# Two-branch block: when a P.V. step's second part is issued, and where the softmax divisions stand

## The chip, the cores and the metric

The kernel runs on one core of one Trainium2 chip. The metric is the device time of one execution in microseconds; the median of 3 runs before the change is 2034.26 (2032.95 to 2034.44). The engines are PE (matrix multiplication), DVE (vector), ACT (activations and copies), POOL (element-wise work and masks) and SP, which here only issues transfers.

## What is computed

All inputs are float32; S = 2048 tokens, D = 576, 32 heads of 18, FH = 2304.

```python
xn = layernorm(x)
# branch A: sliding-window attention, window 256
q, k, v = heads(xn @ wqkv)
p = softmax(where(0 <= i - j < 256, q @ k.T * 18 ** -0.5, -1e9))
s = (p @ v) @ wo
# branch B: a gated MLP with a token mixer
z = gelu(xn @ w_in); z1, z2 = z[:, :FH], layernorm(z[:, FH:])
g = silu((z1 * (w_sp @ z2 + b_sp[:, None])) @ w_out)
out = x + s * g
```

## The kernel before

Every matrix product is made from operands split into a high and a low part, in two or three passes. The kernel goes through its stages in order: normalisation and the q, k, v and z2 products (to about 510 us of the profile), attention together with the z1 product (to about 1036 us), the out-projection (to about 1106 us), the token mixer (Strassen-like products, L1278 on) and the last product with w_out.

The change lies in the attention stage (L895 to L1013). Its work is cut into 16 units (`UNITS`, L24): 8 groups of four heads, first for the lower half of the tokens, then for the upper. For a unit `u` there are five kinds of work:

- maxima: `max_item` (L484) makes a block of scores on PE and takes its row maximum on DVE; 32 per unit. `max_split` and `max_end` (L506, L516) split the maxima into high and low, transpose them on PE, copy them on DVE (`mhl`) and move them by four transfers into rows of the q operand, so that the later scores come out with the maximum already subtracted. The scores of a unit wait for that move.
- scores: `scores` (L606) makes the transposed scores of one head and one key block on PE, ACT takes their exponential (L625), and POOL masks the two edge blocks of all four heads (L633, L636). When four heads are done, the key block goes to the list `todo`.
- P.V.: `pv` (L639) multiplies a key block with the values, for four heads, into an accumulator `ops` of which there is one (`bufs=1`) and which holds four query blocks (`c`). A key block whose queries reach over the end of an accumulator is done in two parts: the second part goes to the list `later` (L656). When an accumulator is full, ACT copies it into half of the tile `ou` (L662; two buffers), and the second parts get the planned end of that copy as their time (L664).
- the end of a unit: `finish` (L669). The values have a column of ones, so `ou` holds the denominators too. A transfer gathers them (`den`, L713), DVE takes the reciprocal (L676), a transfer writes it to memory (`r_d`, L679), another reads it back broadcast to all rows (`rp`, L685; one buffer), DVE multiplies the two halves of `ou` with it (L692; here called the division), and four transfers store the result (`o_d`, L702).
- fill: `z1_rows` (L556), the z1 product. Its matmuls use one half of PE's rows (`ma` or `mb`), as the scores and maxima do, so two run at a time. They are put in wherever nothing else is ready.

The order on all engines is written out by the kernel while it is built (`manual_schedule`). A planner (L962 on) keeps a clock and the planned busy time of ACT, DVE and POOL, and at each step emits what is due: functions registered with `after(ns, fn)` when the clock reaches them (`tick`, L462), then P.V. steps if `pv_now` says so, then a score or a maximum, else fill. Each engine executes its own list in the order in which the planner emitted it, and SP issues its transfers in that order too. So a planned time fixes only a place in the lists; on the chip an instruction waits at that place for what it needs, and what stands behind it waits too.

`pv_now` (L941) counts the entries of `todo` that are due, and `pv_run` (L948) takes that many from the head. After a step that ends an accumulator, the second parts are put at the head of `todo` (L956).

The last unit (u = 15) is treated apart: its tile is `oul`, and its division is made in the out-projection stage (L1052 on). The out-projection's weights are loaded and split during unit 15 (`load_wo`, L885), into buffers of `ou` and `vg` among others (L1003). The tokens' attention results are loaded back by `wo_load` (L872) into `spare` and the operand buffers of heads that are done, and split into `ohl` (L1030), whose memory was `ou` and others of the attention stage.

Of the kernel before, what the change touches and what calls it, by code (L numbers as in the profile page):

```python
# [42 lines left out]
GUARD = 150  # L43
LOAD_NS = 4000
MAX_NS = 3500
WARM = 54


# [9 lines left out]
def kernel(  # L58
# [14 lines left out]
    act, dve, pool, pe, sp = nc.scalar, nc.vector, nc.gpsimd, nc.tensor, nc.sync  # L73
# [154 lines left out]
    with ExitStack() as early:  # L228
# [5 lines left out]
        def pair_banks():  # L234

            turns.append(0)
            return [(fillp, widep)[len(turns) % 2].tile([P, 512], F32, name=n) for n in ("ma", "mb")]
# [6 lines left out]
        with ExitStack() as ph:  # L244
# [104 lines left out]
            warm_up = pair_banks()  # L349
            for n in range(WARM):  # L350
                pe.transpose(warm_up[n // 4 % 2][:, n % 4 * P:(n % 4 + 1) * P], ident, ident)
# [65 lines left out]
        with ExitStack() as ph:  # L417
# [34 lines left out]
            clock = 0.0  # L452
            row_time = [0.0, 0.0]

            def after(ns, fn):
                waiting.append((clock + ns, fn))

            busy = {"act": 0.0, "dve": 0.0, "pool": 0.0}
# [57 lines left out]
            def max_end(u):  # L516
# [14 lines left out]
                for i in range(4):  # L531
                    after(wait + 100 * i, lambda: to_move[u] and to_move[u].pop(0)())
                max_ready[u] = clock + wait + 400 + MAX_NS

# [64 lines left out]
            vgs, pts, left, o_ps, ous, last, todo, later = {}, {}, {}, {}, {}, [], [], []  # L599
# [39 lines left out]
            def pv(u, kb, qa, qz):  # L639
                g, half = UNITS[u]  # L640
                pt = pts[u, kb]
                k0 = 0 if half == 0 else 6
                c = qa // 4
                first = max(4 * c - 2, 0)
                if kb == first:
                    o_ps[c] = ops.tile([P, 512], F32, name="ops")
                hi = min(4 * c + 3, qz)
                for j in range(4):
                    pe.matmul(o_ps[c][32 * j:32 * j + 32, (qa - 4 * c) * P:(hi - 4 * c + 1) * P],  # L649
                              vgs[u][:, kb - k0, j * VW:j * VW + 32], pt[:, j, (qa - kb) * P:(hi - kb + 1) * P],  # L650
                              start=kb == first, stop=kb == 4 * c + 3, skip_group_check=True)
                spend_both((hi - qa + 1) * 218)
                if hi == qz:
                    pts.pop((u, kb))
                else:
                    later.append([0.0, u, kb, hi + 1, qz])  # L656
                if kb == 4 * c + 3:
                    if c % 2 == 0:
                        ous[u] = (ap_.tile([P, HS], F32, name="ou", bufs=2) if u < NU - 1 else
                                  aa.tile([P, HS], F32, name="oul", bufs=1))  # L660
                    ou = ous[u]
                    act.activation(ou[:, c % 2 * 512:c % 2 * 512 + 512], o_ps.pop(c), AF.Copy)  # L662
                    free_at = use("act", 630)
                    for t in later:  # L664
                        t[0] = free_at
                    if c % 2 == 1:
                        finish(u, ou)

            def finish(u, ou):  # L669

                g, half = UNITS[u]
                cs = slice(half * HS, half * HS + HS)
                den = aa.tile([P, HS // 32], F32, name="den")
                rp = ap_.tile([P, HS], F32, name="rp", bufs=1) if u < NU - 1 else f32(slots[4][:, 0:HS])
                def put_inverse():
                    dve.reciprocal(den, den)  # L676
                    t = use("dve", 350) - clock + 300
                    after(t if u < NU - 1 else 0,
                          lambda: sp.dma_start(r_d[u].rearrange("h (a b) -> (h a) b", b=HS // 32), den))  # L679
                    if u == NU - 1:  # L680
                        tick()
                    return t

                def get_inverse():
                    sp.dma_start(rp, r_d[u].unsqueeze(1).to_broadcast([4, 32, HS]))  # L685

                def invert():
                    after(put_inverse() + 4800, get_inverse)

                def divide_half(a):  # L690
                    hs = slice(a * 512, a * 512 + 512)
                    dve.tensor_tensor(ou[:, hs], ou[:, hs], rp[:, hs], ALU.mult)  # L692
                    use("dve", 750)

                def divide():
                    if u == NU - 1:
                        divide_half(0)
                    divide_half(1)

                    def store(i):  # L700
                        h = 4 * g + i
                        sp.dma_start(o_d[h * DH:(h + 1) * DH, cs], ou[32 * i:32 * i + DH, :])  # L702

                    for i in range(4):
                        if u == NU - 1:
                            store(i)
                        else:
                            after(busy["dve"] - clock + 200 + 400 * i, partial(store, i))

                if u == NU - 1:  # L710
                    last.extend([lambda: sp.dma_start(den, ou[DH::32, :]), put_inverse, get_inverse, divide])
                else:
                    after(busy["act"] - clock + 300, lambda: sp.dma_start(den, ou[DH::32, :]))  # L713
                    after(6000, invert)
                    after(16000, partial(divide_half, 0))
                    after(18000, divide)

            def sp_combos(stack):

# [175 lines left out]
            with ExitStack() as heads:  # L895
# [43 lines left out]
                    return head_ready.get(2 * u + j // 2, 1e9) <= clock and done_max[-2] + GUARD <= clock  # L939

                def pv_now():  # L941
                    n = sum(1 for t in todo if t[0] + GUARD <= clock)
                    if n >= 2 or (n and not score_queue[0] and not score_queue[1]):
                        size = sum(t[4] - t[3] + 1 for t in todo[:n])
                        return n if size >= 4 or len(pts) >= 4 or not score_queue[0] else 0
                    return 0
# [15 lines left out]
                while score_queue[0] or score_queue[1] or todo or filling:  # L962
                    r = 0 if row_time[0] <= row_time[1] else 1
                    clock = row_time[r]
# [5 lines left out]
                    n = pv_now()  # L970
# [21 lines left out]
                    u, n, j = score_queue[r].pop(0)  # L992
# [3 lines left out]
                    n = n * 4 + j  # L996
# [3 lines left out]
                        wo_splits.pop(0)()  # L1000
                    if u == NU - 1 and n % 4 == 0 and n // 4 < 5:
                        if n == 0:
                            wors = [aa.tile([P, D], F32, name="wor", bufs=1),  # L1003
                                    ap_.tile([P, HS], F32, name="ou", bufs=2)[:, :D]]
                        if n == 8:
                            wors.append(ap_.tile([P, 10, 89], F32, name="vg").rearrange("p a b -> p (a b)")[:, :D])
                        load_wo(n // 4)
# [10 lines left out]
        with ExitStack() as ph:  # L1018
# [33 lines left out]
            den_load, put_inverse, get_inverse, divide = last  # L1052
# [5 lines left out]
            for n in range(NS):  # L1058
                t, c = divmod(n, 2)
# [264 lines left out]
    with ExitStack() as ph:  # L1324
# [26 lines left out]
        for n, tc_ in enumerate(CH):  # L1351
# [4 lines left out]
            for i in range(2):  # L1356
                final = n + 1 == len(CH) and i == 1
                t = 2 * tc_ + i
# [99 lines left out]
```

## Time and profile before

| | us |
|---|---|
| median of the runs | 2034.26 |
| profiled execution | 2030.1 |
| its span, from the first to the last instruction | 2028.4 |
| attention stage, about | 520 to 1036 |

Over the span PE is busy for 1915.5 us (94%), its weight loads for 1641.3 (81%), DVE for 1074.0 (53%), ACT for 901.4 (44%) and POOL for 344.5 (17%). The mean granted clock of PE is 0.976.

In the rows of the profile, L649 is the line of kernel.py, `out<-in` names the tiles, and a bracket gives the idle time of the engine before the instruction and what ended it. A row of waits reads: engine, tile and line that waited, what it waited for, microseconds in total, number of times, the longest. A row of stretches reads: start and end, length, busy time (and instructions) of PE, PEld, DVE, ACT and POOL, then the granted clock of PE as a share of full speed, the busy share of the DMA engines, and GB/s. PEld is the loading of weights, which overlaps PE. A row of SPq is SP issuing a transfer. Matmuls overlap, so their starts tell more than their lengths.

### The profile page before, as it was taken

What the parts mean: (1) busy time and instruction counts of PE and PEld (TensorE: products, weight loads), DVE (VectorE), ACT (ScalarE), POOL (GpSimd) and SP (SyncE); (2) the same over time, 40 slices, a digit from 0 to 9 for tenths busy, and PEclk for the clock granted to TensorE, in tenths of its full rate; (3) what the DMA queues carried; (4) which work ended last, traced back from release to release, by engine and by line L of the source; (5) the groups of instructions that cost most, each with busy time, mean ns of one, the idle gap of its engine ahead of it and who ended that gap; (6) DMA issues with size and microseconds to landing.
All of it is one profiled execution on the core that took longest, in us unless ns stands there. A gap on an engine that the chain in (4) does not pass through costs nothing.

```text
span 2028.4 us, 38400 instructions
## 1 busy us (share of the span) xinstructions
PE 1915.5 (94%) x14552; PEld 1641.3 (81%) x14552; DVE 1074.0 (53%) x2317; ACT 901.4 (44%) x1746; POOL 344.5 (17%) x421
## 2 busy tenths in 40 slices
PE   6887999998988898999999999999999999999999
PEld 6877999998666666666779888888888888899998
DVE  7511143436665665655522777756777576753332
ACT  3321322222545555555645856546555544442221
POOL 3220143433433333433410000000000000000000
PEclk8998999998999999999999999999999999999999
DMA  6666487887545555556457867766577655685451
GB/s 203 187 154 143 130 266 263 277 260 239 147 125 158 152 154 152 143 149 154 128 175 247 274 217 244 254 233 231 180 242 245 205 173 186 224 259 167 134 158 55
DMA packets 233354, 389.84 MB, mean 192 GB/s; under 512 B 51025, under 2 KB 144721, under 8 KB 233041
## 3 DMA queue, kind: packets, MB, share of 16 engines
q1 hardware_dynamic: 233168, 387.39, 62.1%
q8 instruction: 114, 1.87, 0.4%
q14 instruction: 72, 0.58, 0.1%
HBM read 274.74 MB, written 111.78 MB: 191 GB/s over the span
## 4 chain that ended last, share of the span: by engine, by line
PE 69%; DMA 15%; DVE 6%; SPq 4%; ACT 3%; issue 2%; POOL 0%; DVEq 0%; ACTq 0%; POOLq 0%
PE acc L1288 30%; PE po L1381 11%; PE mb L199 5%; PE ma L568 5%; PE ma L199 5%; PE mb L568 4%; PE ops L649 3%; PE sp L497 3%; PE tps L621 2%; DMA att<-st_d 2%; DMA rp<-r_d 1%; DMA z1wh<-in_w_z_dram 1%; DVE junk L501 1%; DMA wraw<-in_w_v_dram 1%; DMA den<-ou 1%
## 5 line engine op out<-in xcount | busy, mean ns | idle before, releaser
L1288 PE MATMUL acc<-spl,zh 128*128 128x512 f32 x1008 | 392.6, 390 | 1.2 <-DVE spl L109 1.0
L1288 PE MATMUL acc<-sph,zl 128*128 128x512 f32 x1008 | 392.2, 389 | 0.0
L1288 PE MATMUL acc<-sph,zh 128*128 128x512 f32 x1008 | 392.2, 389 | 0.0
L501 DVE CUSTOM_DVE_ANT_0 junk<-sp,band 128x384 bf16<-128x384 f32 (+1 forms) x512 | 276.0, 539 | 182.2 <-PE sp L497 96.6
L625 ACT ACTIVATE pt<-tps 128x384 f32<-128x384 f32 (+2 forms) x576 | 225.8, 443 | 174.8 <-PE tps L621 98.7
L568 PE MATMUL ma<-b,z1wh 64*128 64x512 f32 x648 | 231.2, 411 | 0.7 <-ACT zt L844 0.4
L568 PE MATMUL mb<-b,z1wh 64*128 64x512 f32 x648 | 230.1, 410 | 0.0
L1288 PEld LDWEIGHTS acc<-spl,zh 128*128 128x128 f32 x1008 | 189.2, 188 | 41.9 <-DVE spl L109 2.9
L109 DVE TENSOR_TENSOR spl<-spr,sph 128x1024 fp32r<-128x1024 f32 x168 | 205.3, 1222 | 31.2 <-ACT sph L108 30.0
L1288 PEld LDWEIGHTS acc<-sph,zl 128*128 128x128 f32 x1008 | 189.2, 188 | 39.4
L1288 PEld LDWEIGHTS acc<-sph,zh 128*128 128x128 f32 x1008 | 189.2, 188 | 39.3
L497 PE MATMUL sp<-att 54*128 54x384 f32 (+1 forms) x512 | 179.9, 382 | 24.1 <-DVE mx L501 19.2
L108 ACT ACTIVATE zh<-b 128x384 fp32r<-128x384 f32 x168 | 87.5, 521 | 232.2 <-PE acc L1288 232.2
L621 PE MATMUL tps<-att 56*128 56x384 f32 (+1 forms) x576 | 168.3, 345 | 10.5 <-DMA att<-mhl 10.1
L108 ACT ACTIVATE sph<-spr 128x1024 fp32r<-128x1024 f32 x168 | 175.9, 1047 | 1.3 <-DMA spr<-in_w_sp_dram 0.8
L109 DVE TENSOR_TENSOR zl<-b,zh 128x384 fp32r<-128x384 f32 x168 | 93.0, 553 | 147.8 <-ACT zh L108 142.1
L1381 PE MATMUL po<-b,yh 128*128 128x288 f32 x840 | 147.2, 295 | 0.5 <-ACT gs L1368 0.5
L497 PEld LDWEIGHTS sp<-att 54*128 54x128 f32 x512 | 92.1, 191 | 68.6 <-DVE mx L501 44.0
L568 PE MATMUL ma<-b,z1wl 64*128 64x512 f32 x324 | 131.9, 407 | 0.0
L568 PE MATMUL mb<-b,z1wl 64*128 64x512 f32 x324 | 131.7, 407 | 0.0
L633 POOL TENSOR_SCALAR_AFFINE_SELECT pt<-pt 128x512 f32<-128x512 f32 x128 | 81.9, 640 | 288.3 <-ACT pt L625 286.2
L568 PEld LDWEIGHTS ma<-b,z1wh 64*128 64x128 f32 x648 | 121.8, 194 | 8.8 <-issue 3.1
(222 smaller groups left out, 4332.3 us busy)
## 6 DMA issues: line engine op xcount, KB each, us to landing
spr<-sc_d SPq DMA_DIRECT2D x96, 512.0 KB
spr<-in_w_sp_dram SPq DMA_DIRECT2D x72, 512.0 KB
zr<-z_d SPq DMA_DIRECT2D x144, 192.0 KB
z_d<-zt SPq DMA_DIRECT2D x48, 384.0 KB
z_d<-z1o SPq DMA_DIRECT2D x72, 256.0 KB
z1t<-z_d SPq DMA_DIRECT2D x72, 256.0 KB
y_d<-z1t SPq DMA_DIRECT2D x72, 256.0 KB
a<-in_w_sp_dram SPq DMA_DIRECT2D x64, 256.0 KB
```

The costliest lines, as they stand in the source:

```text
L108: act.activation(hi, src, AF.Copy)
L109: dve.tensor_tensor(lo, src, f32(hi), ALU.subtract)
L199: pe.matmul(banks[h][:, :n], *both[h][i], start=i == 0, stop=i == STEPS - 1)
L497: pe.matmul(ps[:, :w], q_of(u, j)[0:54, i * P:(i + 1) * P], k_of(u, j)[0:54, k0:k0 + w], start=True, stop=True)
L501: dve.tensor_tensor_reduce(out=junk[:, :w], in0=ps[:, :w], in1=band[:, m0:m0 + w], scale=1.0, scalar=-3.0e38, op0=ALU.add, op1=ALU.max, ac ...
L568: pe.matmul(ps, w, x_, start=n == 0, stop=n == STEPS - 1)
L621: pe.matmul(ps[:, :m * P], k_of(u, j)[:, (kb - base) * P:(kb - base + 1) * P], q_of(u, j)[:, (a - lo) * P:(a - lo + m) * P], start=True, s ...
L625: act.activation(pt[:, j, d0:d0 + n * P], ps[:, (qa - a) * P:(qa - a + n) * P], AF.Exp, scale=scale)
L633: pool.affine_select(out=pt[:, :, 0:P], in_=pt[:, :, 0:P], pattern=[[0, 4], [1, P]], compare_op=ALU.is_ge, fill=0.0, base=0, channel_multi ...
L649: pe.matmul(o_ps[c][32 * j:32 * j + 32, (qa - 4 * c) * P:(hi - 4 * c + 1) * P], vgs[u][:, kb - k0, j * VW:j * VW + 32], pt[:, j, (qa - kb) ...
L1288: pe.matmul(acc[j], z[:, ps], w[:, cs], start=s == i == 0 and n in OPENS, stop=s == 7 and i == 2, skip_group_check=True)
L1381: pe.matmul(po[i][:, a, :288], y if ahead else y[:, i * P:(i + 1) * P], w[a], start=f == 0 and m == 0, stop=f == NF - 1 and m == 2)
```

## The change

`pv_now` counts only the entries at the head of `todo` that are due one after the other, up to the first that is not. A second part at the head that waits for its copy thus holds back all of P.V. until the planned end of that copy; before, other entries that were due let it be issued at once.

In `finish`, the reciprocal is registered 8000 ns after the end of a unit (6000 before), and the two halves of the division at 24000 and 26000 ns (16000 and 18000 before). The fetch of `rp` still comes 4800 ns after the reciprocal's planned end. The divisions and the stores of a unit stand in a list `parts[u]`, and each registered call takes the next one from it. Where the planner is about to write `ou` of unit u, or to use an `ou` buffer for the out-projection's weights, it first emits all that is left of unit u - 2.

```diff
+DIVIDE_AT = (24000, 26000)
@@ pv
                 if kb == 4 * c + 3:
                     if c % 2 == 0:
+                        while parts.get(u - 2):
+                            part(u - 2)
                         ous[u] = (ap_.tile([P, HS], F32, name="ou", bufs=2) if u < NU - 1 else
                                   aa.tile([P, HS], F32, name="oul", bufs=1))
...
+            parts = {}
+
+            def part(u):
+                if parts[u]:
+                    parts[u].pop(0)()
@@ finish
                         if u == NU - 1:
                             store(i)
                         else:
-                            after(busy["dve"] - clock + 200 + 400 * i, partial(store, i))
+                            parts[u].append(partial(store, i))
+                            after(busy["dve"] - clock + 200 + 400 * i, partial(part, u))
...
                     after(busy["act"] - clock + 300, lambda: sp.dma_start(den, ou[DH::32, :]))
-                    after(6000, invert)
-                    after(16000, partial(divide_half, 0))
-                    after(18000, divide)
+                    after(8000, invert)
+                    parts[u] = [partial(divide_half, 0), divide]
+                    for ns in DIVIDE_AT:
+                        after(ns, partial(part, u))
@@ pv_now
-                    n = sum(1 for t in todo if t[0] + GUARD <= clock)
+                    n = next((i for i, t in enumerate(todo) if t[0] + GUARD > clock), len(todo))
                     if n >= 2 or (n and not score_queue[0] and not score_queue[1]):
@@ the planner's loop
                     if u == NU - 1 and n % 4 == 0 and n // 4 < 5:
                         if n == 0:
+                            while parts.get(u - 2):
+                                part(u - 2)
                             wors = [aa.tile([P, D], F32, name="wor", bufs=1),
                                     ap_.tile([P, HS], F32, name="ou", bufs=2)[:, :D]]
```

Since the planner's clock moves on with all that it emits, the order of the other work in the stage shifts as well, from unit 1 on.

## The prediction

> **What bounds the kernel now.** I read the stretches first, then the waits of TensorE and VectorE in the attention stage, then single rows around the longest gaps.
>
> ```profile
> 520.00:1036.00 516.00, 467.22 (x4251) 337.91 (x4250) 291.53 (x1013) 284.90 (x707) 188.57 (x278) 0.96 0.53 146
> 1036.00:1106.00 70.00, 65.35 (x461) 63.32 (x460) 16.38 (x21) 30.19 (x42) 0.00 (x0) 0.98 0.74 234
> 1106.00:2028.40 922.40, 916.53 (x4753) 796.62 (x4751) 562.08 (x820) 439.24 (x673) 0.00 (x0) 1.00 0.63 204
> ```
>
> The columns are the stretch, its length, busy time of PE, PEld, DVE, ACT and POOL, the granted clock, and the DMA share. PE is busy for 467.22 of the 516 us that the change touches and the next busiest engine for 337.91 (its own weight loads) or 291.53 (DVE). PE executes a fixed order, so every gap of PE adds to the end: 48.8 us of gaps, and a clock of 0.96, are all that this change can win here. After 1106 PE is 99% busy at full clock, and a shift of the stage before it arrives unshortened. PE's waits and two of DVE's in the stage:
>
> ```profile
> PE sp L497 <- DVE mx L501: 18.2, 13, 3.4
> PE ops L649 <- ACT ou L662: 10.5, 11, 1.4
> PE tps L621 <- DMA att<-mhl: 10.1, 7, 2.6
> PE sp L520 <- DVE ms L511: 5.6, 4, 3.4
> PE ops L649 <- POOL pt L636: 2.4, 3, 0.8
> ```
>
> ```profile
> DVE ou L692 <- DMA rp<-r_d: 17.8, 7, 4.5
> DVE den L676 <- DMA den<-ou: 12.1, 6, 3.6
> ```
>
> Half of the gaps (18.2 + 5.6) is PE waiting for a maximum. DVE is not overloaded: it waits itself, for the broadcast reciprocals (rp) and for the denominators (den), and the maxima stand behind those two instructions in its queue. The rows show it:
>
> ```profile
> PE sp L497 <- DVE mx L501: 7.5, 5, 2.7
> ...
> 717.62 0.68 PE L497 MATMUL sp<-att 54*128 54x384 f32 x1 [3.39 <-DVE mx L501]
> ...
> 793.64 0.42 PE L520 MATMUL sp<-ident,ms 128*64 128x128 f32 x1 [3.39 <-DVE ms L511]
> ...
> 816.19 0.44 PE L497 MATMUL sp<-att 54*128 54x384 f32 x1 [1.26 <-DVE mx L501]
> ...
> 887.42 0.45 PE L497 MATMUL sp<-att 54*128 54x384 f32 x1 [1.73 <-DVE mx L501]
> ...
> 956.97 0.68 PE L497 MATMUL sp<-att 54*128 54x384 f32 x1 [2.14 <-DVE mx L501]
> ```
>
> The first line is the stretch 600:700, where four divisions waited for rp; 793.64 follows a division too. The rows at 717.62, 816.19, 887.42 and 956.97 come right after a reciprocal that waited for den. So divisions cost PE 7.5 + 3.4 = 10.9 us, and reciprocals 3.39 + 1.26 + 1.73 + 2.14 = 8.5 us. Why den is late:
>
> ```profile
> 873.99 0.65 ACT L662 ACTIVATE ou<-ops 128x512 f32<-128x512 f32 x1
> ...
> 880.89 0.62 SPq L713 DMA_DIRECT2D den<-ou  x1
> ...
> 886.59 0.35 DVE L676 RECIPROCAL den<-den 128x32 f32<-128x32 f32 x1 [2.87 <-DMA den<-ou]
> ```
>
> The copy that ends the unit starts at 873.99; den is issued 6.9 us later, because a burst of key and query loads stands ahead of it on SP, and takes 5.7 us more.
>
> Gaps also cost clock:
>
> ```profile
> 716.00:720.00 4.00, 2.38 (x15) 1.35 (x17) 1.91 (x7) 0.51 (x2) 1.62 (x3) 0.67 0.51 152
> 720.00:724.00 4.00, 4.00 (x27) 2.97 (x27) 2.27 (x8) 0.91 (x3) 1.01 (x1) 0.50 0.29 79
> 724.00:728.00 4.00, 4.00 (x52) 3.09 (x46) 1.73 (x7) 1.89 (x7) 0.68 (x2) 0.97 0.15 61
> ```
>
> After the gap before 717.62 the clock is halved: (0.33 + 0.50 + 0.03) x 4 = 3.4 us of PE's work is lost. The same view has such a stretch after the gaps before 793.64, 887.42 and 956.97: four that go back to divisions and reciprocals.
>
> **The change part by part.**
>
> Second parts. `pv_now` now counts only from the head, so a second part that waits for its copy is no longer issued early. The trace has no PE gap at that place: the eleven waits for the copy stand elsewhere.
>
> ```profile
> 649.82 0.53 PE L649 MATMUL ops<-pt,vg 128*32 128x384 f32 x4 [0.81 <-ACT ou L662]
> ```
>
> At 649.82 PE has waited for the copy that ends a unit (directly behind it SP fetches that unit's den), and all eleven waits fall on such a copy: the next unit's first step follows in the same run and needs the one accumulator. That case is untouched; its steps are in `todo`, not in `later`. In the built order the next unit's first step follows directly at 14 of 15 unit ends before and at 10 after, since the planned order has shifted. The waits are 10.5 + 2.4 = 12.9 us (the three put down to POOL stand at such ends too), 0.92 each: -3.7 us, bounds 0 and -12.9. The number of P.V. runs, each with its change of PE's layout, is 87 before and 86 after: nothing. Scores that wait longer for a pt buffer are covered by the z1 matmuls, whose number is unchanged; without that cover it would be a copy's 0.6 us at each of 16 second parts, at most 10 us.
>
> Divisions later. rp is fetched 2 us later and divided 8 us later, so the division has 6 us more; the longest wait was 4.5. I take all 10.9 us as gone; bounds 0 (rp as late as the division) and -10.9. In the new order no division stands between the maxima's split and its transposition; before, three units had that. The divisions now stand behind the first 0 to 14 maxima of the next unit. Two of 0.69 us per unit (the row at 1032.33 below has two in 1.29) were among them before too, and DVE is busy for 291.53 of 516 us: 0; if DVE had no idle time there, 15 x 1.4 = 21 us.
>
> Reciprocals later by 2 us, the mean of the six den waits (12.1 / 6). The longest was 3.6 and the one shown 2.87, of which 1.6 and 0.9 stay; I put what stays in the four units above at 3.7 us on DVE together, of which PE felt 70% (8.5 of about 12): 2.7. But the new order puts stores of the unit before, or long runs of loads, directly ahead of den on SP in eight units instead of four: twice 2.7 = 5.4. Net 5.4 - 8.5 = -3.1; bounds -8.5 and, if eight units wait like the four, +8.5. Queued behind the four stores, should their division be late, are den, the loads for later heads and the moves of the maxima.
>
> Clock. Of the four half-clock stretches I take three as gone, one den gap staying long enough: -10.2; bounds 0 and -13.6. Here the Trainium skill speaks against the change. "TensorE: Matmul & The Clock Gate", section "HAM oscillation — how this bites in real kernels", gives as the abstract rule that gaps should not exceed some 3.4 us. By it only the two gaps of 3.39 would matter, two stretches would go, and the sum would be 3.4 us smaller. The gaps of 1.73 and 2.14 were followed by half clock as well, so I go by the rows.
>
> The end of the stage. Unit 14's chain (denominator, reciprocal, broadcast, division, stores) is on the path, because the first out-projection operand takes the memory of `ou` and waits for those stores:
>
> ```profile
> 1010.58 0.59 ACT L662 ACTIVATE ou<-ops 128x512 f32<-128x512 f32 x1
> ...
> 1037.39 1.27 ACT L1034 ACTIVATE ohl<-spare 128x1280 fp32r<-128x1280 f32 x1 [1.21 <-DMA o_d<-ou]
> ```
>
> ```profile
> 1019.42 0.34 DVE L676 RECIPROCAL den<-den 128x32 f32<-128x32 f32 x1
> 1021.33 0.97 DVE L109 TENSOR_TENSOR att<-vg,att 128x576 fp32r<-128x576 f32 x1 [1.56 <-ACT att L108]
> ...
> 1032.33 1.29 DVE L692 TENSOR_TENSOR ou<-ou,rp 128x512 f32<-128x512 f32 x2 [4.38 <-DMA rp<-r_d]
> ```
>
> ```profile
> 1039.98 0.40 PE L1048 MATMUL wops<-att,ohl 128*128 128x288 f32 x1 [0.46 <-DVE ohl L1035]
> ...
> 1058.45 3.76 PE L1048 MATMUL wops<-att,ohl 128*128 128x288 f32 x15 [3.30 <-DVE ohl L1035]
> ```
>
> In the new order the reciprocal stands behind the split of `vg`, so at 1021.33 + 0.97 = 1022.30 instead of 1019.42: the chain is 2.9 us longer. The thirteen z1 matmuls of one row half that ran after the last P.V. and covered it now stand ahead of it, and the stores stand behind six loads on SP. PE will idle some 8 to 10 us there and pay one half-clock stretch: +2.9 + 3.4. The gap of 3.30 before 1058.45 (DVE held by unit 15's division) should then be covered, and its lower clock (1.7 us by the same view) with it: -5.0. Net +1.3; bounds -2 and +6.3.
>
> What is late next. With DVE on time PE meets sooner what was second: the move of the maxima (10.1 in seven waits), which hangs on SP. I give back a third of 10.9 + 3.1: +4.7, bounds 0 and +14.
>
> Sum: -3.7 - 10.9 - 3.1 - 10.2 + 1.3 + 4.7 = -21.9. The profiled execution (2030.1, span 2028.4) would be 2008.2; the median of the runs lies 4.2 above it, 2034.26, and becomes 2012.4.
>
> **Rivals.**
>
> Slower: the store loop. On SP the four stores wait for the division and den of the next unit waits behind them; a late den makes a late reciprocal, a late rp and a late division, and the lateness comes round again. For it: SP already waits for den and rp in the rows above, and eight den fetches now have such work ahead. Against it: the 6 us of margin. Price per unit: a wait as the longest, 4.5, of which PE feels 70%, 3.1, and a half-clock stretch, 3.4: 6.5 us. What the change removes in all (10.9 + 8.5 + 13.6 = 33) is eaten by five units; from six on the kernel is slower. With eight: 52 - 33 - 3.7 + 1.3 = +16.6, 2050.9.
>
> No change: the move of the maxima takes over. If PE only walks from the maxima's wait into that of the moved maxima, and these gaps keep the clock halved as often, all that remains is -3.7 + 1.3 = -2.4: 2031.9. For it: that wait was 10.1 us with DVE late; against it: the move starts earlier by what DVE gains. That the edit to `pv_now` in itself does nothing, for want of a PE gap at the second parts, is part of my forecast.
>
> Only long gaps cost clock. The two gaps of 3.39 lose a stretch each, the others had another cause: -18.5, 2015.8. This is the reading of the page named above; the rows at 887.42 and 956.97 speak against it.
>
> **How the numbers follow.** About 0.2% (4 us) is what a measurement can tell from no change. The forecast has 0.62, the store loop 0.20, the long-gap case 0.10, no change 0.08. Faster: 0.62 + 0.10 and a little from the third rival's lower side, 0.73; same 0.07; slower 0.20. The forecast's own range is 2002 (all den waits and all four stretches gone, nothing given back) to 2026 (den and clock as before); towards the loop rival the whole range reaches 2042, which leaves out its worse half and a little below 2002.
>
> **What would show it.** Right: DVE's wait for rp under 3 us, PE's for maxima under 10, waits of `ops` for the copy near 9, three or four half-clock stretches fewer between 520 and 1030, a PE gap of 8 us or more before the first out-projection matmuls. Wrong: DVE's den wait above 12, the SP queue's wait for the division above 33, or PE's wait for the moved maxima doubled.

## The result: half a per cent slower, and the profile after

| | us |
|---|---|
| before, median of 9 runs beside it | 2033.82 (2028.07 to 2040.11) |
| after, median of 9 runs | 2040.28 (2036.97 to 2053.72) |
| ratio | 1.0053, 95% interval 1.0033 to 1.0074 |
| profiled execution of after, its span | 2040.28, 2038.6 |

The ratio comes from all runs; the quotient of the two medians alone is 1.0032. The forecast was 2012.4, with a range of 2002 to 2042. The time lies at the range's upper end, and the kernel became slower where it was forecast to become faster. The profiled execution is 10.2 us longer than that of before (2030.1). In kernel.py of after, the lines of the stage up to the scores are those of before plus one. The copy of `ou` is L665, the reciprocal L685, the fetch of `rp` L694, the division L701 and the first out-projection matmul L1061.

Two stretches of after, with the columns of the prediction's first rows:

```profile
520.00:1036.00 516.00, 463.14 (x4181) 342.64 (x4181) 292.06 (x1012) 279.02 (x695) 187.57 (x274) 0.94 0.51 143
...
1116.00:2028.00 912.00, 910.68 (x4714) 791.42 (x4713) 560.57 (x818) 439.81 (x672) 0.00 (x0) 1.00 0.64 207
```

In the same 516 us PE is busy for 4 us less than before, at a clock of 0.94 instead of 0.96, and the last 912 us are full as they were. So the loss lies in the attention stage and its end. PE's waits in 520 to 1060 of after:

```profile
PE tps L622 <- DMA att<-mhl: 18.2, 8, 5.8
PE sp L498 <- DMA att<-st_d: 13.4, 8, 3.4
PE ops L650 <- ACT ou L665: 9.3, 8, 2.7
PE wops L1061 <- ACT ohl L1047: 8.5, 1, 8.5
PE ops L650 <- POOL pt L637: 4.9, 3, 1.9
PE sp L521 <- DVE ms L512: 4.3, 5, 1.3
PE sp L498 <- DVE mx L502: 1.9, 2, 1.7
```

The two waits for maxima, 18.2 + 5.6 us before, are down to 1.9 + 4.3. In their place PE waits for transfers: 18.2 us for moved maxima (10.1 before), and 13.4 for the loads of keys and queries (`att<-st_d`), which were 1.0 before:

```profile
PE sp L497 <- DMA att<-st_d: 1.0, 2, 0.8
```

DVE and SP in the same stretch of after; the first two rows answer the 17.8 and 12.1 of before:

```profile
DVE ou L701 <- DMA rp<-r_d: 6.8, 2, 6.0
DVE den L685 <- DMA den<-ou: 4.0, 2, 3.0
```

```profile
SPq L448 <- DMA rp<-r_d: 18.5, 5, 6.5
SPq L711 <- DVE ou L701: 3.1, 2, 2.6
```

And SP of before, the same two places:

```profile
SPq L447 <- DMA rp<-r_d: 2.9, 1, 2.9
SPq L702 <- DVE ou L692: 32.7, 9, 10.2
```

DVE hardly waits for `rp` any more (6.0 of the 6.8 us are the division of unit 14, at the end of the stage), and SP hardly waits for the division. But SP's loads now wait for `rp` to land. How that looks in the order of time on SP of after, for one unit, and PE at the place where it lacks a load:

```profile
635.40 0.59 SPq L694 DMA_DIRECT2D rp<-r_d  x1
636.43 13.05 SPq L448 DMA_DIRECT2D att<-st_d  x14
649.59 3.01 SPq L528 DMA_DIRECT2D att<-mhl  x4
```

```profile
647.79 0.55 PE L498 MATMUL sp<-att 54*128 54x256 f32 x1 [2.10 <-DMA att<-st_d]
```

The fetch of 512 KB stands directly ahead of fourteen loads. SP takes 13.05 us to issue them, and the moves of the maxima, which stand behind, start only then. Seven of the fourteen are issued from 636.43 to 639.44; the eighth follows at 645.98, after the one wait for `rp` of 6.5 us. The program explains the eighth: as it is built, SP's transfers report their end on eight counters in turn, and the eighth transfer behind `rp` uses rp's counter again and is not issued before rp has landed. So it is the program that holds the loads back, and what counts is how soon the eighth transfer behind rp comes. In the order of after the fetch stands directly ahead of loads in six of 15 units, in that of before in four.

The end of the stage in after:

```profile
1020.91 0.59 ACT L665 ACTIVATE ou<-ops 128x512 f32<-128x512 f32 x1
...
1052.22 1.27 ACT L1047 ACTIVATE ohl<-spare 128x1280 fp32r<-128x1280 f32 x1 [6.49 <-DMA o_d<-ou]
```

```profile
1053.55 2.83 PE L1061 MATMUL wops<-att,ohl 128*128 128x288 f32 x9 [8.47 <-ACT ohl L1047]
```

Unit 14's last copy is at 1020.91 instead of 1010.58, 10.3 us later. The whole execution is 10.2 us longer, so what comes behind that copy costs nothing on balance. But the built order has 15 z1 matmuls more ahead of that copy, and fewer behind it, than before.

### The profile page after: what moved, and what is told of

It is laid out like the page before. It is cut to its first block, busy times and chain, and to the rows that moved or that the text cites. A ratio compares the mean times of both kernels' runs of the same rounds, so it can differ in the third digit from the quotient of the medians.

```text
span 2038.6 us, 38409 instructions
## 1 busy us (share of the span) xinstructions
PE 1916.6 (94%) x14552; PEld 1648.2 (81%) x14552; DVE 1076.2 (53%) x2317; ACT 901.0 (44%) x1746; POOL 346.5 (17%) x421
## 4 chain that ended last, share of the span: by engine, by line
PE 71%; DMA 14%; DVE 5%; SPq 4%; ACT 3%; issue 2%; POOL 1%; DVEq 0%; ACTq 0%; POOLq 0%
PE acc L1301 31%; PE po L1394 11%; PE mb L200 7%; PE ma L569 4%; PE mb L569 4%; PE ops L650 4%; DMA att<-st_d 3%; PE ma L200 3%; PE sp L498 3%; PE tps L622 2%; PE wops L1061 2%; DVE junk L502 1%; DMA att<-mhl 1%; DMA wraw<-in_w_v_dram 1%; DMA sc_d<-a 1%
## 5 line engine op out<-in xcount | busy, mean ns | idle before, releaser
L569 PE MATMUL ma<-b,z1wh 64*128 64x512 f32 x648 | 236.4, 419 | 0.4 <-ACT zt L855 0.4
L569 PE MATMUL mb<-b,z1wh 64*128 64x512 f32 x648 | 234.3, 416 | 0.3 <-ACT z1o L574 0.2
L622 PE MATMUL tps<-att 56*128 56x384 f32 (+1 forms) x576 | 169.5, 353 | 18.9 <-DMA att<-mhl 18.2
L622 PEld LDWEIGHTS tps<-att 56*128 56x128 f32 x576 | 102.2, 198 | 38.4 <-issue 28.6
```

The costliest lines, as they stand in the source:

```text
L569: pe.matmul(ps, w, x_, start=n == 0, stop=n == STEPS - 1)
L622: pe.matmul(ps[:, :m * P], k_of(u, j)[:, (kb - base) * P:(kb - base + 1) * P], q_of(u, j)[:, (a - lo) * P:(a - lo + m) * P], start=True, s ...
```

## The experiments

Ratios are to before in the same call, with the 95% interval. Where an expectation speaks of theory A, it is that the late reciprocal puts rp's transfer onto the burst of loads on SP, so that PE waits for loads and moved maxima.

### The transfer of rp: half of it, or later

rp_half is after with half of the transfer, b_rp_half the same in before. Both leave out the second half of rp and divide all tokens of a unit by the sums of its first half:

```diff
-                    sp.dma_start(rp, r_d[u].unsqueeze(1).to_broadcast([4, 32, HS]))
+                    if u < NU - 1:
+                        sp.dma_start(rp[:, :512], r_d[u][:, :512].unsqueeze(1).to_broadcast([4, 32, 512]))
...
-                    dve.tensor_tensor(ou[:, hs], ou[:, hs], rp[:, hs], ALU.mult)
+                    dve.tensor_tensor(ou[:, hs], ou[:, hs], rp[:, hs] if u == NU - 1 else rp[:, :512], ALU.mult)
```

> The changed kernel with the broadcast of the reciprocals (rp) cut to its first 512 columns, 256 KB instead of 512 KB, for units 0 to 14; both halves of the division multiply with these columns, so the second half of every unit's tokens is divided by the wrong sums. The order on all engines is that of the changed kernel. Theory A (the rp fetch now stands right ahead of the burst of key and query loads, and a load some places behind it on SP waits until rp has landed; loads and moves of the maxima come late): SP's wait of loads for rp falls from 18.5 us to under 8, PE's wait for loads from 13.4 to under 7, time 2030 to 2036. Theory B (the divisions and stores stand in the wrong place, rp does not matter): waits for loads and moved maxima stay within 2 us, time 2038 to 2042.

> The kernel before the change with rp cut to its first 512 columns as in the run rp_half (the second half of every unit's tokens is divided by the wrong sums). The order is that of before. Theory A: the rp fetch does not hold up loads here (2.9 us on SP), so only the divisions' wait shrinks: 17.8 us on DVE falls below 8, time 2022 to 2028. Theory A2: less traffic helps here as much as in the changed kernel, 2015 to 2019.

Measured: rp_half 2024.32, ratio 0.9971 (0.9954 to 0.9989); b_rp_half 2018.04, ratio 0.9918 (0.9889 to 0.9946). The rows of rp_half that moved, PE and SP in 520 to 1060:

```profile
PE tps L622 <- DMA att<-mhl: 13.6, 7, 4.2
...
PE sp L498 <- DMA att<-st_d: 7.9, 5, 4.1
```

```profile
SPq L448 <- DMA rp<-r_d: 3.7, 2, 2.5
```

and DVE in b_rp_half:

```profile
DVE ou L695 <- DMA rp<-r_d: 1.2, 1, 1.2
```

In both kernels the second half of rp costs 0.0082 of the time (1.0053 - 0.9971, and 1 - 0.9918), about 17 us. The waits that fall with it differ: in after SP's for rp (18.5 to 3.7), in before DVE's (17.8 to 1.2). Read by these rows, the change took rp's wait off DVE, as predicted, and paid about the same for it on SP. The times alone do not say it: rp_half is faster than either theory had it, and b_rp_half lies in the range of A2, by which less traffic in itself helps. The difference between the two kernels, 0.0053, is the same with half of rp (0.9971 - 0.9918): the net loss has another cause than rp's length.

rp9800 is after with the fetch 5 us later, all orders but SP's as they were:

```diff
-                    after(put_inverse() + 4800, get_inverse)
+                    after(put_inverse() + 9800, get_inverse)
```

> The changed kernel with the rp fetch emitted 9800 ns instead of 4800 ns after the planned end of the reciprocal; only SP's list changes. The first loads of the burst now stand ahead of rp. Theory A: the loads that PE needs first are no longer behind rp, PE's wait for loads falls below 9 us; the divisions wait for rp instead (over 20 us on DVE in total), time between 2032 and 2042. Theory B: DVE's wait grows and nothing falls, time above 2044.

Measured: 2072.68, ratio 1.0208 (1.0175 to 1.0241). DVE, then SP, in 520 to 1060:

```profile
DVE ou L701 <- DMA rp<-r_d: 32.5, 6, 11.4
```

```profile
SPq L448 <- DMA rp<-r_d: 32.9, 5, 8.0
```

Five microseconds are enough to take both ways at once: DVE waits for rp again, and SP's loads wait still longer. Theory A was wrong here: PE's wait for loads did not fall below 9 us but rose from 13.4 to 16.5, and the time lies where theory B had it. Since only SP's list was moved, rp's place alone is worth 0.0155 here, about 32 us.

### Undoing one part, or taking another way for rp

```diff
@@ inv6: the reciprocal back at 6000
-                    after(8000, invert)
+                    after(6000, invert)
@@ div16: the divisions back at 16000 and 18000
-DIVIDE_AT = (24000, 26000)
+DIVIDE_AT = (16000, 18000)
@@ div245
+DIVIDE_AT = (24500, 26500)
@@ pool_rp: the fetch issued by POOL
-                    sp.dma_start(rp, r_d[u].unsqueeze(1).to_broadcast([4, 32, HS]))
+                    (pool if u < NU - 1 else sp).dma_start(rp, r_d[u].unsqueeze(1).to_broadcast([4, 32, HS]))
@@ tail14: unit 14 alone at the times of before
-                    after(8000, invert)
+                    after(8000 if u < NU - 2 else 6000, invert)
...
-                    for ns in DIVIDE_AT:
+                    for ns in DIVIDE_AT if u < NU - 2 else (16000, 18000):
```

> The changed kernel with the reciprocal back at 6000 ns: late divisions alone. Theory A: rp is out of the burst again, SP's wait of loads for rp under 6 us, no division waits; time 2022 to 2031. Theory B: late divisions and stores are the harm, time 2037 to 2044.

> The changed kernel with the divisions back at 16000 and 18000 ns: the late reciprocal alone. Theory A: rp comes 2 us later into the loads and the division waits longer for it (DVE over 30 us in total): time above 2042. Theory B: as before the change or a little slower by the longer wait, 2034 to 2040.

> The changed kernel with the rp fetch of units 0 to 14 issued by POOL instead of SP; PE, DVE and ACT keep the order of the changed kernel, the amount moved is the same. Theory A (what hurts is that transfers on SP wait until rp has landed): SP's waits for rp are gone, PE's waits for loads under 8 us, time 2018 to 2030, less what POOL's masks lose by standing behind the wait for the written reciprocals. Theory A2 (what hurts is rp's traffic beside the loads): PE's waits for loads and moved maxima stay, time 2036 to 2043.

> The changed kernel with unit 14 alone at the times of before (reciprocal 6000, divisions 16000 and 18000); the order differs only behind the end of unit 14, on SP and by two places on DVE. If the end of the stage pays for the later reciprocal and for the stores behind the loads of the attention results, PE's wait before the out-projection (8.5 us) falls below 5 and the time is 2 to 6 us under the changed kernel's, 2034 to 2038. If the chain is bound elsewhere, 2039 to 2041.

> The changed kernel with the divisions at 24500 and 26500 ns: a small shift that gives another order from unit 1 on. It measures how far the time moves with the order alone. Theory A: rp stands ahead of loads or moved maxima here too, so the time stays 2034 to 2050, with SP's waits of loads or moves for rp above 10 us. If it is below 2030 with such waits, theory A is wrong.

| | median us | ratio |
|---|---|---|
| inv6 | 2059.87 | 1.0134 (1.0098 to 1.0170) |
| div16 | 2076.12 | 1.0219 (1.0194 to 1.0245) |
| pool_rp | 2051.48 | 1.0091 (1.0061 to 1.0120) |
| tail14 | 2043.30 | 1.0047 (1.0030 to 1.0064) |
| div245 | 2055.42 | 1.0110 (1.0077 to 1.0144) |

None was good as an undo, and all but div16 (which theory A had above 2042) lie above every range that was expected of them. inv6 was to bring most of the loss back and lost 0.0081 more, some 16 us. PE, then ACT, in 520 to 1060 of inv6:

```profile
PE tps L622 <- ACT pt L626: 20.2, 6, 6.1
```

```profile
ACT z1wh L584 <- DMA z1raw<-in_w_z_dram: 32.0, 6, 7.7
```

ACT stood before weights of the z1 product that SP had not delivered, 32.0 us in six waits, and PE before ACT's exponentials. Neither kernel of the pair has that wait of PE at more than 0.4 us; div245 has it too, with 14.2 us of PE and 26.5 of ACT. These look like consequences of the shifted order, not of the time of one reciprocal.

div16 keeps only the late reciprocal of the change. PE in 520 to 1060:

```profile
PE sp L498 <- DVE mx L502: 30.1, 12, 6.4
PE sp L521 <- DVE ms L512: 20.1, 8, 4.5
```

Here the division has 2 us less than before instead of 6 more, and PE waits for the maxima for 50 us. The late division is thus needed with the late reciprocal; how much of the 0.0219, some 45 us, is the order's cannot be read here.

pool_rp takes rp off SP, and SP's wait for it is gone. DVE's division waits 25.2 us for rp instead, and PE still waits for moved maxima and loads (18.2 and 13.4 in after):

```profile
rp<-r_d POOLq DMA_DIRECT2D x14, 512.0 KB, 9.7
```

```profile
PE tps L622 <- DMA att<-mhl: 23.8, 14, 4.7
...
PE sp L498 <- DMA att<-st_d: 10.4, 6, 2.8
```

By these waits, if not by its time, it speaks for A2, that rp's traffic hurts beside the loads: SP's loads also wait longer for earlier loads, 32.8 us instead of 22.2. It does not settle it, since it gives back on DVE what it takes off SP. tail14 has the wait before the out-projection at 5.1 us instead of 8.5, but 21.4 us for the moved maxima instead of 18.2, and no gain in all. Up to unit 14 its order is that of after, so such sums of waits differ by 3 us between two executions of one order.

So edits of planned times could not be used as single changes: each one rewrites the order of the whole stage. The next runs keep the order.

### The order of before, kept

The planner books the reciprocal and the divisions as before does, and the instructions come at other times, without being booked:

```diff
@@ keep_div
+                def late_half(a):
+                    hs = slice(a * 512, a * 512 + 512)
+                    dve.tensor_tensor(ou[:, hs], ou[:, hs], rp[:, hs], ALU.mult)
...
                     after(6000, invert)
-                    after(16000, partial(divide_half, 0))
-                    after(18000, divide)
+                    parts[u] = [partial(late_half, 0), late_stores]
+                    for ns in (16000, 18000):
+                        after(ns, lambda: use("dve", 750))
+                    for ns in (24000, 26000):
+                        after(ns, partial(part, u))
@@ keep_all, beside that
-                    after(6000, invert)
+                    after(6000, lambda: use("dve", 350))
+                    after(8000, invert_late)
```

PE's and POOL's lists are those of before, instruction by instruction, `pv_now` of after included. nb161 and nb165 do the reverse: before, with the divisions planned 100 or 500 ns later, which on DVE means nothing in itself.

```diff
-                    after(16000, partial(divide_half, 0))
-                    after(18000, divide)
+                    after(16100, partial(divide_half, 0))
+                    after(18100, divide)
```

> Before's order on PE and POOL, instruction for instruction: the planner books the divisions at 16000 and 18000 ns as before, but emits them and their stores at 24000 and 26000; the reciprocal stays at 6000. Only DVE's and SP's lists move (and two operands at the end on ACT). Theory C (the later division does what it is for, and the shifted order of everything else ate it): DVE's wait for rp under 3 us, PE's wait for maxima under 12, time 2014 to 2026. Theory D (the stores, now later on SP, hold up loads and moves): waits for loads and moved maxima 8 us or more above before's 11, time 2034 or more.

> The same with the reciprocal emitted at 8000 ns too, booked at 6000: all that the change moves, in before's order of PE and POOL. Theory C: the den wait falls from 12 to under 7 as well, time 2010 to 2024. Theory D: 2036 or more.

> The kernel before with the divisions planned 100 ns later (16100, 18100). Nothing is meant by it; it gives another order from some unit on. Theory C: the order alone moves the time by several microseconds either way, 2026 to 2060, by SP's deliveries (moved maxima, loads). Theory D: within 4 us of before.

> The kernel before with the divisions planned 500 ns later (16500, 18500); as nb161. Theory C: 2026 to 2060, another value than nb161. Theory D: within 5 us of before.

| | median us | ratio |
|---|---|---|
| keep_div | 2022.33 | 0.9952 (0.9934 to 0.9971) |
| keep_all | 2029.57 | 0.9994 (0.9975 to 1.0013) |
| nb161 | 2072.09 | 1.0181 (1.0136 to 1.0226) |
| nb165 | 2060.95 | 1.0134 (1.0092 to 1.0177) |

keep_div is faster than both kernels. PE's waits in 520 to 1060 of keep_div, then DVE's and SP's for rp:

```profile
PE sp L498 <- DVE mx L502: 10.1, 8, 3.0
PE tps L622 <- DMA att<-mhl: 8.7, 7, 2.8
PE wops L1086 <- ACT ohl L1072: 5.7, 2, 3.9
PE sp L498 <- DMA att<-st_d: 3.6, 3, 1.5
```

```profile
DVE ou L706 <- DMA rp<-r_d: 7.4, 2, 4.6
```

```profile
SPq L448 <- DMA rp<-r_d: 1.3, 1, 1.3
```

The late division does what the prediction said of it, though DVE's wait is not under the 3 us that were expected: it is 7.4 instead of 17.8, the maxima's 10.1 instead of 18.2, and nothing of that size has taken their place (the loads rose from 1.0 to 3.6, the operands of the out-projection from 3.8 to 6.2). That late stores harm is refuted with it. keep_all has the late reciprocal as well, and loses 7.2 us of the 9.4; its time lies between the two ranges expected. Its PE and SP rows:

```profile
PE tps L622 <- DMA att<-mhl: 19.5, 9, 4.6
...
PE sp L498 <- DMA att<-st_d: 7.7, 4, 2.5
```

```profile
SPq L448 <- DMA rp<-r_d: 12.6, 4, 6.7
SPq L528 <- DMA rp<-r_d: 3.1, 1, 3.1
```

(Its profiled execution, 2038.5, is the longest of its ten, so the rows show it at its worst.)

nb161 loses 40 us and nb165 29, for edits that move nothing on purpose. PE in 520 to 1060 of nb161:

```profile
PE tps L621 <- ACT pt L625: 12.3, 5, 6.5
...
PE ops L649 <- POOL pt L636: 11.3, 2, 10.5
PE sp L497 <- DMA att<-st_d: 9.7, 5, 3.8
```

One wait of 10.5 us for a mask and exponentials that come late are new; ACT waits 24.7 us for z1 weights. nb165 loses in another way: DVE waits 30.7 us for rp, and PE 20.8 for maxima. Both times lie above the range of theory C, which had expected less of the order. The planner books ACT, DVE and POOL, but not when SP's transfers land, so a neutral shift can put work where its operand is not there yet.

### What the late reciprocal costs: its place, or rp's

```diff
@@ keep_all_rp28: keep_all, the fetch 2800 ns after the store
-                    after(650 + 4800, get_inverse)
+                    after(650 + 2800, get_inverse)
@@ keep_div_rp33: keep_div, the fetch 1500 ns earlier
-                    after(put_inverse() + 4800, get_inverse)
+                    after(put_inverse() + 3300, get_inverse)
@@ keep_div_t: keep_div, unit 14 as in before (keep_div20_t: and 20000, 22000 elsewhere)
-                    for ns in (24000, 26000):
+                    for ns in ((24000, 26000) if u < NU - 2 else (16000, 18000)):
```

> Order of before on PE and POOL, reciprocal emitted at 8000 and divisions at 24000 and 26000 as in keep_all, but rp is fetched 2800 ns after the reciprocal's store instead of 4800, so that it stands on SP about where keep_div has it, mostly ahead of other things than the burst of loads. Theory A (the late reciprocal costs by putting rp's transfer onto the burst of loads): SP's loads wait for rp under 6 us in all (12.6 in keep_all), PE waits for the moved maxima 8 to 13 us (19.5), time 2020 to 2026. Rival (the late reciprocal costs in itself, by a late rp for the division or by DVE's order): time 2027 to 2033, and DVE's wait for rp stays near 7 us.

> keep_div with rp fetched 3300 ns after the reciprocal's planned end instead of 4800. Theory A (rp's place on SP sets what its transfer falls on): rp now starts 1.5 us earlier, DVE's wait for rp falls from 7.4 to under 4 us, SP's loads wait for rp no more than in keep_div (1.3 us), and SP waits a little for the reciprocals to be stored; time 2016 to 2022. Rival (rp was not what DVE and SP were short of; the fetch now only blocks SP while the store is under way): time 2022 to 2028.

> keep_div, but unit 14's divisions at 16000 and 18000, so that its stores stand ahead of the loads of the attention results as in before. Theory (the stage's end in keep_div costs what the wait of the out-projection for its first operand shows): that wait falls from 5.7 us to about 1, time 2015 to 2019 against 2022.3 of keep_div. Rival (the end is set by something else): the wait stays or moves to another operand, time 2020 to 2025.

> Order of before on PE and POOL, divisions at 20000 and 22000 (unit 14 at 16000 and 18000), reciprocal at 6000. If four microseconds more are enough to take the division's wait for rp off DVE (longest 4.5 us before): time 2015 to 2021, DVE's wait for rp under 9 us, PE's wait for maxima under 11. If it is the place behind the split maxima that counts and not the time: between before and keep_div, 2022 to 2030.

| | median us | ratio |
|---|---|---|
| keep_all_rp28 | 2026.24 | 0.9971 (0.9948 to 0.9995) |
| keep_div_rp33 | 2025.67 | 0.9962 (0.9942 to 0.9981) |
| keep_div_t | 2022.83 | 0.9944 (0.9924 to 0.9965) |
| keep_div20_t | 2029.80 | 0.9979 (0.9960 to 0.9997) |

In keep_all_rp28 rp's fetch stands directly ahead of loads in four units, as in before and keep_div, instead of six as in keep_all and after. By its ratio it is half of the way back from keep_all to keep_div, though its interval overlaps both. SP:

```profile
SPq L448 <- DMA rp<-r_d: 8.1, 2, 4.9
SPq L528 <- DMA rp<-r_d: 2.3, 1, 2.3
```

Its waits for rp fell only from 15.7 to 10.4 us, PE still waits 17.2 us for moved maxima, and the time lies between the two ranges: the cause was not taken away, so it is no clean test. In keep_div_rp33 DVE's wait fell from 7.4 to 5.2 us, less than theory A expected, and the time did not fall: the rival was right, rp's place has no more to give there. In keep_div_t the wait for the first out-projection operand fell from 5.7 to 1.9 us, but other operands of it are late by 3.4 in two waits, and the time is that of keep_div, as the rival said. keep_div20_t has the waits that the first theory expected (4.4 us for rp on DVE, 9.4 for maxima on PE) but the time of the other: it gains less than half of what keep_div does. What takes the rest is open; PE's wait for loads is 6.5 us there, against 3.6.

The last pair is the cleanest test of the point. keep_div and keep_all with half of rp, every order kept:

```diff
-                    sp.dma_start(rp, r_d[u].unsqueeze(1).to_broadcast([4, 32, HS]))
+                    n = 512 if u < NU - 1 else HS; sp.dma_start(rp[:, :n], r_d[u][:, :n].unsqueeze(1).to_broadcast([4, 32, n]))
```

> keep_div with half of rp: only the first 512 columns are fetched (256 KB instead of 512) and both halves are divided by them, so the second half of the tokens of every unit but the last is divided by wrong sums. All orders of keep_div, SP's too. It is the base for keep_all_half. With the half transfer DVE's wait for rp (7.4 us) goes; both theories: 2012 to 2021.

> keep_all with half of rp, wrong sums likewise, all orders of keep_all. Keep_all stands 7.2 us above keep_div with the whole rp. Theory A (what the late reciprocal costs is that loads and moves on SP wait for the long transfer of rp): SP's waits for rp fall from 15.7 to under 4 us, and the distance to keep_div_half falls under 3 us. Rival (the late reciprocal costs in itself, by where it and the divisions stand among DVE's maxima): the distance to keep_div_half stays at 5 to 9 us. Something between says that both have a share.

Measured: keep_div_half 2022.35, ratio 0.9929 (0.9898 to 0.9960), just above its range; keep_all_half 2014.25, ratio 0.9894 (0.9864 to 0.9924). PE and SP of keep_all_half:

```profile
PE sp L498 <- DMA att<-st_d: 7.8, 5, 2.3
PE tps L622 <- DMA att<-mhl: 7.8, 6, 2.8
```

```profile
SPq L448 <- DMA rp<-r_d: 0.9, 1, 0.9
```

The distance of 7.2 us between the two is gone; it is -8.1, with intervals that overlap. SP's waits for rp fell from 15.7 to 0.9 us, and PE's wait for moved maxima from 19.5 to 7.8. (Part of that fall is the choice of executions: keep_all's profile is of its slowest, this one, 2010.75, of one of its fastest. The medians of six and seven runs carry the point.) So the late reciprocal costs nothing in itself that these runs can tell; its price hangs on rp's long transfer, for which loads and moves on SP wait. In keep_div, where SP waits 1.3 us for rp, the half transfer brings nothing that these runs can tell (0.9952 and 0.9929, intervals that overlap). So less traffic alone is not what helps; whether rp's bytes beside the loads cost something on top of the wait on SP stays open, since the half transfer shortens both. All ratios to before in one table:

| | rp whole | rp half |
|---|---|---|
| before | 1 | 0.9918 |
| keep_div (division late) | 0.9952 | 0.9929 |
| keep_all (reciprocal late too) | 0.9994 | 0.9894 |
| after (the same times, the order shifted) | 1.0053 | 0.9971 |

Between keep_all and after lies 0.0059 with the whole rp and 0.0077 with half, 12 and 16 us: the price of the shifted order, which does not depend on rp's length as far as these runs can tell (each of the two differences is uncertain by about 0.003).

## Why the prediction was wrong, point by point

- **Second parts (-3.7).** The kernel before with this edit alone builds to the same lists on all engines, as the forecast had it; but the shifted order did not save waits at the unit ends either: 10.5 + 2.4 us before, 9.3 + 4.9 after, +1.3.
- **Divisions and reciprocals (-10.9 and -3.1).** Right, and the gain forecast was somewhat low. PE's waits for maxima fell by 17.6 us, and DVE's waits for rp and den from 17.8 and 12.1 to 6.8 and 4.0. The first rival, the store loop, did not come: SP's wait for the division went from 32.7 to 3.1 us.
- **The end of the stage (+1.3).** PE's wait of 8 to 10 us was 8.47, and the gap of 3.30 is not there any more. These waits before and in the out-projection grew from 3.8 to 8.5 us, +4.7. That the balance from the last copy of unit 14 to the end is still -0.1 is due to the z1 matmuls that now run ahead of the copy.
- **What is late next (+4.7, bounds 0 and +14).** This is the step that failed most, by size and by kind: measured +20.5, 15.8 us more than forecast. The moved maxima took 8.1 us more, as the second rival had it, and the loads 12.4 us, which no case of the forecast had; together they lie above the upper bound. The step counted only who would come second in the old order. Of the reciprocal's move it priced the den fetch's neighbours on SP, not those of the rp fetch, though rp's fetch moves with it.
- **Clock (-10.2).** The second term that failed, and it rests on the first: the gaps did not go, but moved, and the lower clock with them. PE's clock in 520 to 1036 went from 0.96 to 0.94. Summed as the prediction did it, (1 - clock) x 4 over the 4 us windows from 520 to 1036, 18.8 us were lost before and 30.8 after. How much of this the time felt is not known: PE is busy for 487.4 us from 520 to 1060 in before, and for 488.3 in the same piece of after, which is 10.2 us longer. After the gap of 2.10 at 647.79 the clock is halved:

```profile
643.00:647.00 4.00, 2.56 (x15) 1.57 (x14) 2.97 (x10) 1.09 (x2) 0.00 (x0) 0.97 0.25 89
647.00:651.00 4.00, 3.21 (x16) 3.24 (x18) 1.60 (x5) 0.00 (x0) 0.00 (x0) 0.50 0.66 182
651.00:655.00 4.00, 3.13 (x14) 2.18 (x13) 0.43 (x2) 1.13 (x3) 0.00 (x0) 0.50 0.35 107
```

  So the third rival, that only long gaps cost clock, has this row against it as well. The Trainium skill ("TensorE: Matmul & The Clock Gate", section "HAM oscillation — how this bites in real kernels") gives as its abstract rule that PE should have no idle gaps over some 3.4 us; read as if shorter gaps cost nothing, it does not agree with this row.

- **Hardly in the sum: the order.** The text ahead of the prediction says that the order of the stage shifts. The sum priced this in three places (the unit ends, what stands ahead of den, the end of the stage) and took the rest of the shift at nothing, without a reason. Against before, the gaps of PE ahead of unit 14's last copy grew by -17.6 + 1.3 + 20.5 = +4.2 us, and those of the out-projection's operands by 4.7: together 8.9 of the 10.2 us. With the order kept the same times of reciprocal and division give 0.9994. The shift is therefore what makes the kernel slower on balance; the transfer of rp, moved with the reciprocal, is what eats most of the division's gain. Seven planned orders other than that of before were run (after, inv6, div16, tail14, div245, nb161, nb165), and all are slower than it, by 0.5 to 2.2%, two of them with edits that mean nothing. How much of the seven is chance is not known; which place in after's order costs the 12 us was not shown. The waits for loads, for POOL's masks and before the out-projection are each longer in after's trace than in that of keep_all, but these two executions are only 1.7 us apart, so their rows cannot say it.

Of the signs named for "wrong", den and the division's stores went the right way, and the wait for moved maxima came near to double (10.1 to 18.2). Of those named for "right", the waits for maxima, for the copy and before the out-projection came as said; DVE's wait for rp, 6.8 us, and the clock did not. Two slips of the prediction change nothing in this: its lower end, worked from its own terms, is 1998.9 and not 2002, and of the four divisions that it has waiting for rp between 600 and 700 the profile puts one, at 632.48, down to a load.

## What to carry to other kernels

When a planner writes the order, a changed time is two changes: the one that is meant, and a new order of everything behind it. Price the second one too, by a shift that means nothing, and try the first with the old order booked: here the late division alone, in the old order, gave 0.9952 where the change gave 1.0053. And when a long transfer moves, look at what stands behind it in the list of its queue, here up to the eighth place: a wait taken off DVE came back through the same transfer on SP, for about the same price.

## What was not expected of the hardware

- In this program a fetch of 512 KB holds up the eighth transfer issued behind it until it has landed. Fourteen loads took 13.05 us to issue right behind rp in after, and 10.98 in rp_half, where the fetch has 256 KB. In keep_div, behind four other transfers that came after rp, fourteen loads took 6.83:

```profile
595.86 0.59 SPq L694 DMA_DIRECT2D rp<-r_d  x1
599.79 2.68 SPq L528 DMA_DIRECT2D att<-mhl  x4
603.09 6.83 SPq L448 DMA_DIRECT2D att<-st_d  x14
```

- A shift of 100 ns in two planned places made the execution 40 us longer (nb161), more than the 23.8 us that PE waits for maxima in before.
- The same fetch issued by POOL took 7.6 to 14.7 us from its issue to its landing, with a median of 9.7. Issued by SP in before, it took 7.9 to 9.7 us to the start of the division in the seven places where the profile has the division wait for it.
